# Newton rounds of the early RMS norms on GpSimd, halves of the squares added there, pairs 2 and 3 normalized singly, first exponents earlier

## The chip, the cores and the metric

The kernel runs on one core of a Trainium2 chip. The core has five engines with instruction queues of their own: TensorE (PE, with its weight loads PEld), VectorE (DVE), ScalarE (ACT), GpSimd (POOL) and SyncE (SP, which here only issues DMAs). Each runs its queue strictly in order and waits on semaphores of the others. The metric is device time in microseconds (us), the median of several executions. One execution with the hardware profiler gave the profile.

## The reference

Three stages in a row, all in float32; the MLP's weights arrive as 64-bit floats, and the kernel converts them itself.

```python
# q, k, v: (4 batches, 12 heads, 448 positions, 64)
rms = np.sqrt(np.mean(x * x, axis=-1, keepdims=True) + 1e-06)
q_n, k_n = q / rms_q * g_q, k / rms_k * g_k
scores = (1 / 8) * q_n @ k_n.T              # per head, 448 x 448
attn = np.exp(scores - max); attn = attn / (attn.sum() + 1e-09)
x = (attn @ v) -> (1792, 768)
h = x @ w_in                                # 768 -> 2048
x = (h * np.clip(h + 3, 0, 6) / 6) @ w_out  # 2048 -> 768
# capacity MoE: logits = x @ w_gate; greedy assignment, 224 tokens for each of 8 experts
out[expert e's tokens] = np.maximum(x @ w1[e], 0) @ w2[e]
```

## The kernel before

The 48 (batch, head) units are worked on as 24 pairs of heads, `i` = 0 to 23, six to a batch. Pairs 0 to 5 are the first batch. Nothing of the MLP can run beside them, since it needs all heads of a batch; from the second batch on, MLP matmuls of the batch before fill PE between the attention steps. Beside the first batch, DVE and ACT also convert `w_in` from 64 bits to 32 (`conv`, lines 140 to 143, tile `cv`, which has one buffer: the next conversion waits until the store of the last one has landed).

For each pair: squares of q and k on ACT (`sq`, two buffers), their sums over 64 columns on DVE (`sums`, L253: 16 sums per position-partition, 8 for q and 8 for k); the inverse root from a bit-trick guess (L257, L258) and three Newton rounds of three small dependent instructions (L260 to L262) on DVE (`invert`); the scaling of q and k on GpSimd (`norm`, L273, tile `xn`, one buffer each for q and k); transposes on PE (`transp`, L290), split into a rounded high part on ACT (`qh`, `kh`) and a low part on DVE (`ql`, `kl`, L302); rough scores on PE (`s1`, L313) for the row maxima on DVE (`mx`, L316, eight per pair); the maxima transposed (`mt`, L322) and spread by DVE (`mr`, L324); exact transposed scores (`sT`, L335) with that maximum subtracted, exponents on ACT (`ph`, L346), and attention times v on PE (`av`, L375). In the first batch the output's scaling is: row sums (`scol`, L390) and their reciprocal (L395) on DVE, the product on GpSimd (`num`, L396), then transposes on PE (L407).

All PSUM tiles come from one ring of eight banks, in program order.

The order on every engine is written out by hand. Each step of pair `i` has a due time in slots, counted from 16 x `i` (the `T_...` tables); events are sorted by due time, and at each slot the queued MLP matmuls are dealt out between them. So a pair takes 16 slots, and a step's due time alone sets where it stands in every engine's queue. In the table before, `sums` of a pair stand at -50, `invert` at -42, `norm` at -38, the q and k transposes at -30 and -28, `sT` at 0, 0.1, 8, 8.1, and `normalize` (which holds the L395 and L396 instructions) at 28. Pairs 0 and 1 have a Newton chain each; from pair 2 on, two neighbouring pairs share one (`GROUPS`), with 32 columns instead of 16.

Of the kernel before, what the change touches and what calls it, by code (L numbers as in the profile page):

```python
# [8 lines left out]
F32 = mybir.dt.float32  # L9
F32R = mybir.dt.float32r  # L10
BF16 = mybir.dt.bfloat16
I32 = mybir.dt.int32
AF = mybir.ActivationFunctionType
OP = mybir.AluOpType
# [7 lines left out]
def kernel(  # L22
# [14 lines left out]
    nc = tc.nc  # L37
    B, H, S, D = q.shape
# [5 lines left out]
    CP = 112  # L44
    NCH = S // CP
# [9 lines left out]
    SQ = 2  # L55
# [12 lines left out]
    CI, CI0, CI1, CI2, CO = 6, 1.75, 2.5, 0.5, 1.5  # L68

    T_LOAD, T_VLOAD, T_NORM, T_Q, T_K, T_V = -72, -12, -38, -30, -28, 6  # L70
    T_SUMS, T_INV = -50, -42
    T_S1, T_MT = (-24, -23.9, -16, -15.9), -9
    T_ST = (0, 0.1, 8, 8.1)
    T_AV = ((17, 18, 19.5, 20.5), (22, 23, 24.5, 25.5))
# [120 lines left out]
    apool = a_stack.enter_context(tc.tile_pool(name="apool", bufs=2, side="left"))  # L195
# [23 lines left out]
    QKV, OPER, XT, FIRST, TR = {}, {}, {}, {}, {}  # L219
    NH2 = B * H // 2  # L220
# [16 lines left out]

    NST = 2 * 2 * NCH

    GROUPS = [(0,), (1,)] + [(g, g + 1) for g in range(2, NH2, 2)]  # L240
    GROUP = {i: g for g in GROUPS for i in g}
    ST = {}

    def sums(i):

        g = GROUP[i]
        if g not in ST:
            ST[g] = [apool.tile([CP, len(g) * NST], F32, name=f"st{k}_{len(g)}", bufs=2) for k in range(3)]
        o = g.index(i) * NST
        for a in range(2):  # L250
            sq = apool.tile([CP, 2 * NCH, D], F32, name="sq", bufs=SQ)
            nc.scalar.activation(sq, QKV[i][a].rearrange("p h c d -> p (h c) d"), AF.Square)
            nc.vector.tensor_reduce(ST[g][0][:, o + a * 2 * NCH:o + (a + 1) * 2 * NCH], sq, axis=AX.X, op=OP.add)  # L253

    def invert(g):
        ms, y, t = ST[g]
        nc.vector.tensor_scalar(ms, ms, 1.0 / D, 1e-6, op0=OP.mult, op1=OP.add)  # L257
        nc.vector.tensor_scalar(y.bitcast(I32), ms.bitcast(I32), -0.5, 1597463007.0, op0=OP.mult, op1=OP.add)  # L258
        for _ in range(3):
            nc.vector.scalar_tensor_tensor(t, y, -0.5, y, op0=OP.mult, op1=OP.mult)  # L260
            nc.vector.tensor_tensor(t, t, ms, op=OP.mult)
            nc.vector.scalar_tensor_tensor(y, t, 1.5, y, op0=OP.add, op1=OP.mult)  # L262

    def norm(i):
        g = GROUP[i]
        y = ST[g][1][:, g.index(i) * NST:(g.index(i) + 1) * NST]
        n = 2 * NCH
# [438 lines left out]
    def at(t, fn, *args):  # L706
        events.append((t, len(events), fn, args))
# [7 lines left out]
    for i in range(NH // 2):  # L715
        t = 16 * i
        at(t + T_LOAD, load, i)
        at(t + T_VLOAD, vload, i)
        g = GROUP[i]
        first = 16 * g[0]  # L720
        at(first + T_SUMS + 4 * (i - g[0]), sums, i)
        if i == g[-1]:
            at(first + T_INV, invert, g)
        at(t + T_NORM, norm, i)
        at(t + T_Q, transp, i, 0)
        at(t + T_K, transp, i, 1)
        at(t + T_V, vsplit, i)
        for c in range(NCH):
            at(t + (T_S1[c] if i else -24 + 0.1 * c), s1, i, c)
            at(t + T_ST[c], sT, i, c)  # L730
            if i in QMAJOR:
                for s in range(2):
                    at(t + T_AV[s][c], av, i, s, c)
            else:
                at(t + T_PV[c], pv, i, c)
        at(t + (T_MT if i else -21), mt, i)
        if i in QMAJOR:
            at(t + T_NUM, normalize, i)
            at(t + T_XT, xt, i)
        else:  # L740
            for n in range(2):
                at(t + T_ADD[n], padd, i, n)
            for d, fn in ((T_SUM, psums), (T_RS, rs_out), (T_RL, rs_in), (T_REC, rec), (T_RO, r_out), (T_RB, r_in), (T_X, xmul)):
                at(t + d, fn, i)
            at(t + T_XH, xsplit, i, False)
            at(t + T_XL, xsplit, i, True)
        if (i + 1) % NP == 0:
            at(t + T_MLP[i // NP], mlp_next, i // NP)
# [315 lines left out]
    for t in range(NTC):  # L1064
        a, z = t * 128, t * 128 + 128
# [137 lines left out]
    for pi, (t, hfs) in enumerate(passes):  # L1203
# [10 lines left out]
        for f in range(NF):  # L1214
            i, k = divmod(f, QF)
# [139 lines left out]
```

## Time and profile before

| | us |
|---|---|
| runs of the kernel, median of 3 | 1167.9 (1166.67 to 1169.88) |
| the profiled execution's own time | 1170.09 |
| its span, first to last instruction | 1168.3 |
| busy in the span: PE | 1104.3 (95%) |
| DVE | 716.6 (61%) |
| ACT | 518.7 (44%) |
| POOL | 426.3 (36%) |

PE is busy nearly throughout, so what PE loses at any place tends to reach the end. In the page's 40 slices of 29 us PE's busy tenths begin 3, 8, 8, 8, 9 and DVE's 7, 8, 8, 7, 8: the first 115 us, the first batch, are where PE has gaps and DVE is fullest.

### The profile page before, as it was taken

To read this page: it belongs to the slowest core of one execution; us is meant where nothing else is said; L and a number is where in the kernel's file an instruction comes from. 1 tells how busy PE (TensorE), PEld (TensorE's weight loads), DVE (VectorE), ACT (ScalarE), POOL (GpSimd) and SP (SyncE) were. 2 spreads that over 40 slices of the span, in tenths; PEclk is the share of its full clock that TensorE was granted. 3 is DMA by queue.
4 is the path that set the end of the run, shared out by engine and by line. 5 is a ranking of instruction groups with operands and counts; after the bars stand their busy time and mean duration, and the time that the engine had idled before them with its cause. 6 is when DMAs were issued, how large, how long until landed. Compare 5 with 4: busy or idle time off the path is not lost.

```text
span 1168.3 us, 19514 instructions
## 1 busy us (share of the span) xinstructions
PE 1104.3 (95%) x7253; PEld 908.8 (78%) x7253; DVE 716.6 (61%) x1493; ACT 518.7 (44%) x941; POOL 426.3 (36%) x317
## 2 busy tenths in 40 slices
PE   3888989999999999999999999999998899999997
PEld 2777756756766666788777888888877899999997
DVE  7887887886667755213440666666665866666560
ACT  3655645644545546544452111111114765656551
POOL 2322455664444532213353000000004676865550
PEclk9998989999999999999999999999998899999999
DMA  4465898978677777759996323222237887877731
GB/s 122 119 190 137 251 293 262 311 236 313 219 240 237 251 263 260 231 195 305 312 350 188 80 61 83 69 82 69 72 91 198 232 259 227 253 228 220 227 127 41
DMA packets 212679, 230.96 MB, mean 198 GB/s; under 512 B 26276, under 2 KB 185704, under 8 KB 212584
## 3 DMA queue, kind: packets, MB, share of 16 engines
q1 hardware_dynamic: 209256, 218.71, 60.9%
q0 software_dynamic: 3328, 11.01, 3.1%
q8 instruction: 57, 0.93, 0.3%
q14 instruction: 38, 0.31, 0.1%
HBM read 178.63 MB, written 51.04 MB: 197 GB/s over the span
## 4 chain that ended last, share of the span: by engine, by line
PE 69%; DVE 10%; DMA 9%; issue 5%; ACT 4%; POOL 2%; SPq 1%; POOLq 0%; DVEq 0%; ACTq 0%
PE y L1155 19%; PE h L528 15%; PE y L1307 8%; PE h L1243 6%; PE st L335 4%; PE h L1245 3%; PE av L424 3%; PE av L375 2%; DMA w_hl<-w 2%; DMA sum_dr<-rb 2%; DVE cv L142 1%; PE rt L948 1%; PE lg L570 1%; DVE mx L316 1%; ACT ph L346 1%
## 5 line engine op out<-in xcount | busy, mean ns | idle before, releaser
L528 PE MATMUL h<-xh,w 128*128 128x448 f32 x768 | 242.3, 386 | 2.8 <-DVE mr L324 2.3
L528 PEld LDWEIGHTS h<-xh,w 128*128 128x128 f32 x768 | 144.5, 192 | 38.6 <-issue 22.2
L528 PE MATMUL h<-xl,w 128*128 128x448 f32 x384 | 146.7, 382 | 0.0
L316 DVE TENSOR_REDUCE mx<-s 112x1 f32<-112x448 f32 x192 | 105.8, 612 | 41.6 <-PE s L313 41.5
L1093 ACT ACTIVATE g2h<-gr 128x512 fp32r<-128x512 f32 x60 | 37.7, 631 | 205.9 <-PE y L1155 160.5
L1155 PE MATMUL y<-woh,g2l 128*128 128x512 f32 (+1 forms) x448 | 125.1, 345 | 1.2 <-POOL g2l L1058 1.2
L1155 PE MATMUL y<-woh,g2h 128*128 128x512 f32 (+1 forms) x448 | 125.4, 345 | 0.0
L1155 PE MATMUL y<-wol,g2h 128*128 128x512 f32 (+1 forms) x448 | 125.1, 344 | 0.0
L118 DVE TENSOR_TENSOR wel<-we_s,weh 128x768 fp32r<-128x768 f32 x59 | 89.3, 1520 | 55.6 <-ACT weh L117 43.7
L117 ACT ACTIVATE weh<-we_s 128x768 fp32r<-128x768 f32 x107 | 88.3, 841 | 63.1 <-DMA we_s<-in_moe_w_dram 45.5
L118 POOL TENSOR_TENSOR wel<-we_s,weh 128x768 fp32r<-128x768 f32 x48 | 97.3, 2031 | 49.8 <-ACT weh L117 36.4
L346 ACT ACTIVATE ph<-st 112x448 f32<-112x448 f32 x192 | 92.6, 543 | 41.6 <-PE st L335 40.7
L1243 PE MATMUL h<-xe,weh 128*128 128x448 f32 x318 | 102.2, 381 | 3.7 <-DVE xe L1194 3.7
L1058 POOL TENSOR_TENSOR g2l<-gr,g2h 128x512 fp32r<-128x512 f32 x14 | 18.2, 1304 | 232.3 <-ACT g2h L1093 232.2
L417 POOL TENSOR_TENSOR pa<-ph 112x448 f32<-112x448 f32 x68 | 84.7, 1267 | 47.4 <-ACT ph L346 47.4
L528 PEld LDWEIGHTS h<-xl,w 128*128 128x128 f32 x384 | 74.0, 193 | 12.3 <-issue 7.0
L1155 PEld LDWEIGHTS y<-woh,g2h 128*128 128x128 f32 x448 | 72.0, 189 | 10.8 <-issue 1.5
L1155 PEld LDWEIGHTS y<-woh,g2l 128*128 128x128 f32 x448 | 72.0, 189 | 10.7 <-POOL g2l L1058 1.4
L1155 PEld LDWEIGHTS y<-wol,g2h 128*128 128x128 f32 x448 | 71.9, 189 | 9.1 <-issue 0.7
L531 ACT ACTIVATE r<-h,half 128x448 f32<-128x448 f32 x64 | 40.6, 635 | 83.2 <-PE h L528 73.0
L1245 PE MATMUL h<-xe,wel 128*128 128x224 f32 x318 | 77.5, 271 | 0.0
L1307 PE MATMUL y<-weh,hl 128*112 128x384 f32 x216 | 72.9, 338 | 0.0
(245 smaller groups left out, 2346.7 us busy)
## 6 DMA issues: line engine op xcount, KB each, us to landing
we_s<-in_moe_w_dram SPq DMA_DIRECT2D x128, 384.0 KB
w<-w_hl SPq DMA_DIRECT2D x32, 768.0 KB
gr<-g_dr SPq DMA_DIRECT2D x52, 256.0 KB
wraw<-in_moe_w_in_dram SPq DMA_DIRECT2D x16, 768.0 KB
win_v<-w SPq DMA_DIRECT2D x32, 384.0 KB
w_hl<-w SPq DMA_DIRECT2D x16, 768.0 KB
wraw<-in_moe_w_out_dram SPq DMA_DIRECT2D x16, 768.0 KB
g_dr<-g SPq DMA_DIRECT2D x48, 224.0 KB
```

Of the source, the lines that this page charges most:

```text
L117: nc.scalar.activation(hi, raw, AF.Copy)
L118: eng.tensor_tensor(lo, raw, hi.bitcast(F32), op=OP.subtract)
L316: mx = nc.vector.tensor_reduce(MX[i][:, s, c:c + 1], pp[s][:CP, :S], axis=AX.X, op=OP.max)
L335: nc.tensor.matmul(pp[s][:CP, :S], a[r], b[r], start=(n == 0), stop=(n == len(todo) - 1))
L346: nc.scalar.activation(e, pp[s][:CP, :S], AF.Exp)
L417: nc.gpsimd.tensor_tensor(PA[i, s, n], PP[i, s, 2 * n][0], PP[i, s, 2 * n + 1][0], op=OP.add)
L528: nc.tensor.matmul(p[:, :S], lhs[:, c], x[:, c], start=(n == 0), stop=(n == 3 * NC - 1))
L531: nc.scalar.activation(r, p[:, :S], AF.Relu, bias=half, scale=1.0 / 6.0)
L1155: nc.tensor.matmul(pp[hf][:, :COLS[hf].stop - COLS[hf].start], a[:, f % QF], w[:, COLS[hf]], start=(f == 0 and n == 0), stop=(f == NF - 1 ...
L1243: mm = [lambda: nc.tensor.matmul(p[:, :4 * CP], wh[:, fo], x.rearrange("d k t -> d (k t)"), start=(c == 0), stop=(c == NC - 1), skip_group ...
L1245: lambda: nc.tensor.matmul(p[:, :2 * CP], wl[:, fo], x[:, 0], start=False, stop=False, skip_group_check=True)]
L1307: nc.tensor.matmul(p[:CP, :HW], a[:, f, tk], w[:, o], start=(f == 0 and n == 0), stop=(f == FB - 1 and n == 2))
```

## The change

For pair groups that begin at pairs 1 to 9, the three Newton rounds move from DVE to GpSimd, where a round takes four instructions (the fused DVE forms are written out). The guess stays on DVE. Pairs 2 and 3 now form groups of their own. For the groups (4,5), (6,7), (8,9) the rounds stand at -35.5, just behind `normalize` of the pair four before, and the scaling of the group's first pair right behind them at -35.4. For pairs 2 to 9 GpSimd first adds the two halves of each pair's squares (`fold`), so that DVE sums 32 columns instead of 64; squares, fold and sums now stand at three due times. The first pair's exact scores and exponents move from slots 0, 0.1, 8, 8.1 to -9, -8.9, 1, 1.1.

```diff
-    GROUPS = [(0,), (1,)] + [(g, g + 1) for g in range(2, NH2, 2)]
+    GROUPS = [(g,) for g in range(4)] + [(g, g + 1) for g in range(4, NH2, 2)]
+    def squares(i):
+        for a in range(2):
+            SQS[i, a] = apool.tile([CP, 2 * NCH, D], F32, name="sq", bufs=SQ)
+            nc.scalar.activation(SQS[i, a], QKV[i][a].rearrange("p h c d -> p (h c) d"), AF.Square)
+
+    def fold(i):
+        for a in range(2):
+            sq = SQS[i, a]
+            nc.gpsimd.tensor_tensor(sq[:, :, :D // 2], sq[:, :, :D // 2], sq[:, :, D // 2:], op=OP.add)
+            SQS[i, a] = sq[:, :, :D // 2]
+    def guess(g):                       # the two instructions that invert() began with, on DVE
+    def invert(g):
+        ms, y, t = ST[g]
+        if 0 < g[0] < NG0:              # NG0 = 10
+            p = nc.gpsimd
+            for _ in range(3):
+                p.tensor_tensor(t, y, y, op=OP.mult)
+                p.tensor_tensor(t, t, ms, op=OP.mult)
+                p.tensor_scalar(t, t, -0.5, 1.5, op0=OP.mult, op1=OP.add)
+                p.tensor_tensor(y, y, t, op=OP.mult)
+            return
-        at(first + T_SUMS + 4 * (i - g[0]), sums, i)
+        t_sq = first + T_SUMS + 4 * (i - g[0])
+        at(t_sq, squares, i)
+        if 2 <= i < NG0:
+            at(t_sq + 2, fold, i)
+            t_sq += 3
+        at(t_sq, sums, i)
+        late_g = 4 <= g[0] < NG0
         if i == g[-1]:
-            at(first + T_INV, invert, g)
-        at(t + T_NORM, norm, i)
+            at(t_sq if 2 <= i < NG0 else first + T_INV, guess, g)
+            at(first + (T_INV0 if late_g else T_INV), invert, g)     # T_INV0 = -35.5
+        at(t + (T_INV0 + 0.1 if late_g and i == g[0] else T_NORM), norm, i)
-            at(t + T_ST[c], sT, i, c)
+            at(t + (T_ST[c] if i else (-9, -8.9, 1, 1.1)[c]), sT, i, c)
```

On GpSimd before, around the output scaling of pair 0 (`num`): the scalings of pair 4 (`xn_615`, `xn_617`) stand ahead of it.

```order
L273 TENSOR_TENSOR xn_428<-ld_q,st_2_252 112x2x4x64
L273 TENSOR_TENSOR xn_430<-ld_k,st_2_252 112x2x4x64
L273 TENSOR_TENSOR xn_615<-ld_q,st_2_433 112x2x4x64
L273 TENSOR_TENSOR xn_617<-ld_k,st_2_433 112x2x4x64
L396 TENSOR_TENSOR num<-num,scol 112x512
L273 TENSOR_TENSOR xn_792<-ld_q,st_2_433 112x2x4x64
```

On GpSimd now, the same place: the folds of pairs 4 and 5, `num` of pair 0, and behind it the first of three Newton rounds of pairs 4 and 5.

```order
L254 TENSOR_TENSOR sq<-sq 112x8x32 x4
L419 TENSOR_TENSOR num<-num,scol 112x512
L277 TENSOR_TENSOR st_2_514<-st_2_513 112x32
L278 TENSOR_TENSOR st_2_514<-st_2_514,st_2_512 112x32
L279 TENSOR_SCALAR st_2_514<-st_2_514 112x32
L280 TENSOR_TENSOR st_2_513<-st_2_513,st_2_514 112x32
```

On GpSimd now, eight rows on, the end of the third round and what stands behind it: the scalings of pair 4 (`xn_653`, `xn_655`) and 5.

```order
L278 TENSOR_TENSOR st_2_514<-st_2_514,st_2_512 112x32
L279 TENSOR_SCALAR st_2_514<-st_2_514 112x32
L280 TENSOR_TENSOR st_2_513<-st_2_513,st_2_514 112x32
L296 TENSOR_TENSOR xn_653<-ld_q,st_2_513 112x2x4x64
L296 TENSOR_TENSOR xn_655<-ld_k,st_2_513 112x2x4x64
L296 TENSOR_TENSOR xn_826<-ld_q,st_2_513 112x2x4x64
L296 TENSOR_TENSOR xn_828<-ld_k,st_2_513 112x2x4x64
```

So pair 4's scaling moved from ahead of `num` to behind it and behind twelve dependent instructions; pairs 6 and 8 stand the same way behind `num` of pairs 2 and 4.

On DVE before, ahead of pair 2's `mr`: two of the conversion's instructions with the guess and, in between, the Newton rounds of pairs 4 and 5 (the first is shown).

```order
L390 TENSOR_SCALAR scol<-av,eps 112x4
L141 TENSOR_SCALAR cv<-cv 128x768
L257 TENSOR_SCALAR st_2_432<-st_2_432 112x32
L258 TENSOR_SCALAR st_2_433<-st_2_432 112x32
L260 SCALAR_TENSOR_TENSOR st_2_434<-st_2_433 112x32
L261 TENSOR_TENSOR st_2_434<-st_2_434,st_2_432 112x32
L262 SCALAR_TENSOR_TENSOR st_2_433<-st_2_434,st_2_433 112x32
```

On DVE now, the same place: the sums of pair 5's folded squares, the guess, and then `mr` without the nine Newton instructions.

```order
L413 TENSOR_SCALAR scol<-av,eps 112x4
L265 TENSOR_REDUCE st_2_512<-sq 112x8 x2
L269 TENSOR_SCALAR st_2_512<-st_2_512 112x32
L270 TENSOR_SCALAR st_2_513<-st_2_512 112x32
L141 TENSOR_SCALAR cv<-cv 128x768
L142 SCALAR_TENSOR_TENSOR cv<-wraw,cv 128x768
L347 TENSOR_TENSOR mr<-t,place 128x448
```

The nine rows between the guess and `mr` are gone from DVE's queue, here and at the other four groups.

## Rows read from the trace of the kernel before

**Rows 1.** Busy time by stretch: us, then each engine's busy time (instructions), granted clock, DMA

```profile
40.00:50.00 10.00, 8.00 (x64) 6.71 (x65) 8.98 (x25) 4.43 (x9) 3.65 (x3) 0.86 0.20 51
```

**Rows 2.** PE's waits, 0 to 115 us: us in total, times, longest

```profile
PE s L313 <- DVE mr L324: 5.2, 3, 2.3
```

**Rows 3.** DVE in time: start, us, instruction, count, idle before it and what ended it

```profile
13.67 0.18 DVE L260 SCALAR_TENSOR_TENSOR st<-st 112x16 f32<-112x16 f32 x1
...
15.44 4.33 DVE L316 TENSOR_REDUCE mx<-s 112x1 f32<-112x448 f32 x8
...
39.48 1.27 DVE L253 TENSOR_REDUCE st<-sq 112x8 f32<-112x512 f32 x2
...
42.27 0.19 DVE L260 SCALAR_TENSOR_TENSOR st<-st 112x32 f32<-112x32 f32 x1
...
44.19 0.95 DVE L142 SCALAR_TENSOR_TENSOR cv<-wraw,cv 128x768 int32<-128x768 int32 x1
...
49.15 0.20 DVE L395 RECIPROCAL scol<-scol 112x8 f32<-112x8 f32 x1
51.05 0.56 DVE L141 TENSOR_SCALAR cv<-cv 128x768 int32<-128x768 int32 x1 [1.70 <-ACT cv L140]
```

**Rows 4.** DVE in time, the same columns, later in the first batch

```profile
78.91 0.20 DVE L395 RECIPROCAL scol<-scol 112x8 f32<-112x8 f32 x1
...
111.31 0.22 DVE L390 TENSOR_SCALAR scol<-av,eps 112x4 f32<-112x4 f32 x1 [1.87 <-PE av L375]
...
113.25 0.20 DVE L395 RECIPROCAL scol<-scol 112x8 f32<-112x8 f32 x1
```

**Rows 5.** GpSimd in time, the output scalings of pairs 0, 2 and 4

```profile
49.61 1.06 POOL L396 TENSOR_TENSOR num<-num,scol 112x512 f32<-112x512 f32 x1 [1.85 <-ACT num L391]
...
79.42 1.06 POOL L396 TENSOR_TENSOR num<-num,scol 112x512 f32<-112x512 f32 x1 [1.53 <-ACT num L391]
...
113.61 1.63 POOL L396 TENSOR_TENSOR num<-num,scol 112x512 f32<-112x512 f32 x1 [4.55 <-ACT ph L346]
```

**Rows 6.** PE in time: three stalls, and the q transposes of pairs 4, 6, 8

```profile
45.73 0.46 PE L313 MATMUL s<-kh,qh 64*112 64x448 f32 x2 [2.00 <-DVE mr L324]
...
53.58 0.55 PE L290 MATMUL t<-ident,xn 112*128 112x112 f32 x4
...
65.14 0.60 PE L407 MATMUL t<-ident,num 112*128 112x112 f32 x4 [1.29 <-POOL num L396]
...
76.21 0.45 PE L313 MATMUL s<-kh,qh 64*112 64x448 f32 x2 [2.26 <-DVE mr L324]
...
84.03 0.55 PE L290 MATMUL t<-ident,xn 112*128 112x112 f32 x4
...
117.37 0.55 PE L290 MATMUL t<-ident,xn 112*128 112x112 f32 x4
```

**Rows 7.** Granted clock behind two stalls: us, PE's busy time, clock, DMA

```profile
49.00:50.00 1.00, 1.00 (x10) 0.50 0.81 187
66.00:67.00 1.00, 1.00 (x13) 1.00 0.82 192
```

**Rows 8.** GpSimd and DVE lines: count, durations in ns (least, median, most)

```profile
L474 POOL TENSOR_TENSOR xl<-xn_t,xh x17: 1137/1158/2194, 158.3 to 509.7; 128x448 fp32r<-128x448 f32 x17
...
L118 DVE TENSOR_TENSOR w<-win_v,w x16: 946/959/3446, 128.8 to 591.5; 128x768 fp32r<-128x768 f32 x16
...
L118 POOL TENSOR_TENSOR w<-win_v,w x16: 1824/1842/1860, 129.7 to 587.0; 128x768 fp32r<-128x768 f32 x16
```

**Rows 9.** A small GpSimd instruction: busy us, mean ns, idle before

```profile
L845 POOL IOTA ei<- 128x8 int32 x1 | 0.2, 154 | 0.0
```

**Rows 10.** GpSimd in time, one weight split

```profile
138.48 1.83 POOL L118 TENSOR_TENSOR w<-win_v,w 128x768 fp32r<-128x768 f32 x1 [7.01 <-ACT w L117]
```

**Rows 11.** DVE in time beside it, a guess of 32 columns

```profile
139.74 0.61 DVE L257 TENSOR_SCALAR st<-st 112x32 f32<-112x32 f32 x1
140.39 1.08 DVE L258 TENSOR_SCALAR st<-st 112x32 int32<-112x32 int32 x1
```

**Rows 12.** ACT in time, pair 2's output copied out

```profile
78.91 0.38 ACT L391 ACTIVATE num<-av 112x256 f32<-112x256 f32 x1 [3.83 <-DVE scol L390]
```

**Rows 13.** The chain that ended last: start, us, what

```profile
154.00 9.09 DMA w_hl<-w
```

More of the change, by code (lines that the diff above doesn't have):

```diff
@@ L70 @@
     T_LOAD, T_VLOAD, T_NORM, T_Q, T_K, T_V = -72, -12, -38, -30, -28, 6
-    T_SUMS, T_INV = -50, -42
+    T_SUMS, T_INV, T_INV0, NG0 = -50, -42, -35.5, 10
     T_S1, T_MT = (-24, -23.9, -16, -15.9), -9
@@ L238 @@
     NST = 2 * 2 * NCH
-    GROUPS = [(0,), (1,)] + [(g, g + 1) for g in range(2, NH2, 2)]
+    GROUPS = [(g,) for g in range(4)] + [(g, g + 1) for g in range(4, NH2, 2)]
     GROUP = {i: g for g in GROUPS for i in g}
     ST = {}
+    SQS = {}
+    def squares(i):
[7 more added lines that the diff above has]
+            SQS[i, a] = sq[:, :, :D // 2]
     def sums(i):
@@ L250, in sums @@
         for a in range(2):
-            sq = apool.tile([CP, 2 * NCH, D], F32, name="sq", bufs=SQ)
-            nc.scalar.activation(sq, QKV[i][a].rearrange("p h c d -> p (h c) d"), AF.Square)
+            sq = SQS.pop((i, a))
             nc.vector.tensor_reduce(ST[g][0][:, o + a * 2 * NCH:o + (a + 1) * 2 * NCH], sq, axis=AX.X, op=OP.add)
-    def invert(g):
+    def guess(g):
         ms, y, t = ST[g]
```

## The prediction

> **What bounds the kernel now.** I read the page's busy slices first, then the table of stretches, PE's waits, the timelines of DVE, PE and GpSimd, and last the chain of waits. PE is busy for 95% of the span, and from the second batch on MLP matmuls fill its gaps, so only the first batch is in question. There DVE is the fullest engine: from 40 to 50 us it works 8.98 of 10 us, GpSimd 3.65, and PE 8.00 at a granted clock of 0.86 [rows 1]. The sharpest place is pair 2's `mr`: PE waited for such a spread of maxima three times, 5.2 us in all [rows 2]. The timeline says why. At 42.27 DVE begins the Newton rounds of pairs 4 and 5 and is through at 44.19; `mr` stands behind them, and PE's next rough scores start at 45.73 after 2.00 us idle [rows 3, 6]. The same happens at 76.21, with 2.26 us [rows 6]. After the first of these stalls PE has a clock of 0.50 for a while; after a stall of 1.29 us at 65.14 it keeps 1.00 [rows 6, 7]. So a Newton chain on DVE costs its own length and some clock behind it.
>
> **What the change takes off DVE.** A chain of nine is 15.44 - 13.67 = 1.77 us for 16 columns and 44.19 - 42.27 = 1.92 us for 32 [rows 3]; four chains have 32 columns. Two reductions of 512 columns take 1.27 us; a column costs 4.33 / 8 / 448, a little over 1 ns, so halving saves about 0.27 us each, 0.54 per pair [rows 3]. I cut the path at the reciprocals of pairs 0, 2 and 4 (49.15, 78.91, 113.25) [rows 3, 4].
>
> Up to 49.15: Newton 1.77 + 1.92 + 1.92, halves for four pairs 2.2, less one guess more (two instructions of 1.92 / 9) 0.4: 7.4 us off DVE. Not all of it reaches the path, since pairs 1 to 3 now hang on a serial GpSimd queue: Newton, two scalings, two folds. Pair 1's Newton, now begun where DVE's began (13.67), ends at about 16.5, its scalings at 18.6, pair 2's folds at 20.1 (prices below), while DVE is ready for pair 2's sums at about 19.2: it has mx done at 13.67 + 4.33 and `mr` a microsecond later [rows 3]. That wait, with the sum's own place, costs 0.7; PE then runs pair 0's two early exponent sets before pair 1's scores, for which I put 1.0; and 0.3 for each fold of pairs 3 to 5. So 7.4 - 2.6 = 4.8, and I take **4.7 us gained** (between 3.2, if each GpSimd instruction costs what the second rival says, and 7.4). The early exponents themselves cost nothing: ACT has worked 4.43 us of ten even later [rows 1]; what they gain, an earlier release of PSUM banks, I put at nothing, because DVE's eight maxima per pair, 4.33 us, come behind it anyway.
>
> From 49.15 to 78.91: 1.92 and one pair's halves 0.54 (the other pair's stand beside a wait for ACT): **2.5**. From 78.91 to 113.25: 1.92 + 0.54, and the 1.87 us that DVE waited for `av` at 111.31, which ran at half clock behind the Newton stall [rows 4]: **4.3**. In all 11.5 us.
>
> **What it puts behind `num`.** In the order of GpSimd, pair 4's scaling has moved from ahead of pair 0's `num` to behind it and behind twelve instructions, each of which waits for the one before. Behind these wait pair 4's and 5's scalings and the next `num`; PE's q transposes of pair 4 wait for the first of them, and PE is in order, so all of PE waits, and with it DVE's `ql`. No DMA is passed. No row shows GpSimd on 16 or 32 columns. From 448 columns in 1158 ns and 768 in 1842 [rows 8], a column costs 2.14 ns and an instruction 0.20 us: 0.27 us for 32 columns, 0.235 for 16, 0.75 for a fold of 256. The one-input instruction I put at the 0.154 us of the small iota [rows 9]. A chain of twelve is then 9 x 0.27 + 3 x 0.154 = 2.9 us (2.6 for 16 columns). Bounds: all at 0.154, 1.85 us; or with 0.13 us more for each wake, which is what GpSimd took from the end of ACT's copy (79.29) to `num` (79.42) [rows 5, 12], 4.45 us. I take 2.9, the value nearest the rows that compute.
>
> GpSimd and DVE also exclude each other: an instruction of the guess on DVE, of a size that otherwise takes 0.19 us [rows 3], lasted from 139.74 to 140.35, just until GpSimd's split of 138.48 to 140.31 ended, and the next one 1.08 us [rows 10, 11]. So the conversion on DVE, 0.56 + 0.95 us for two instructions [rows 3] and 2.46 for three, holds up the chain where it falls into it: two beside pair 4's chain, all three beside pair 6's, one beside pair 8's.
>
> From a reciprocal's start to the q transposes, now: wait for `num` 0.46, 0.51, 0.36; `num` 1.06, 1.06, 1.63 [rows 5]; chain 2.9; exclusion 1.5, 2.5, 0.95; one scaling 1.1 (it has `num`'s size). Sums 7.0, 8.1, 6.9. Before: 53.58 - 49.15 = 4.4, 84.03 - 78.91 = 5.1, 117.37 - 113.25 = 4.1 [rows 3, 4, 6]. **8.4 us lost.** It doesn't hide: in between PE has only `xt` and one `av` block to do.
>
> **Clock.** PE's new stalls are of over 3 us, longer than the 2.00 that lost the clock. In 40 to 50 us the clock of 0.86 cost 1.4 us [rows 1]; three times that, **4.2 us lost** (nothing, if the stalls stay near 1.29).
>
> Sum: -11.5 + 8.4 + 4.2 = +1.1. On the profiled execution's own 1170.1 us that is 1171.2; its own time stands 2.2 above the median of the runs, so **1169.0**. What a measurement of this kernel can tell from no change is about 0.3%, 3.5 us: the forecast is no change that can be told, 1165.5 to 1172.5.
>
> **Rivals.**
> *The chain is short and the clock stays* (faster). For it: the small iota's 0.154 us, and DVE's fullness [rows 1, 9]. Against it: two-input instructions have an offset of 0.20 by the line through rows 8. With 1.85 us a chain, three tails are 3.2 shorter (5.2), the first leg gains 0.7 more, stalls come near 2 us and the clock holds: -12.2 + 5.2 = -7.0, so 1160.9.
>
> *The Newton chain behind `num` becomes the wait that sets the pair's pace* (slower). At 4.45 us a chain the tails lose 13.0, the first leg gains 3.2 in place of 4.7, so -10.0 + 13.0 + 4.2 = +7.2: 1175.1. It decides from about 0.29 us an instruction on, where the sum passes +3.5. For it: twelve waits in series, and the wake of 0.13. Against it: DVE's own chain loses only 0.02 us between instructions (1.92 / 9 against 0.19) [rows 3]. The Trainium skill's GPSIMD Engine Reference (Elementwise, side-by-side cycle accounting) measures GpSimd at 1.96 times DVE's time for an add and keeps to DVE for elementwise work. At 768 columns this trace has 1842 ns against 959, 1.92 times, as the page says [rows 8]; for 32 columns no run here shows it. By that ratio on DVE's 0.19 us an instruction would be 0.37 us, and the sum that of this rival, as an estimate.
>
> *The difference is swallowed downstream* (no change, 1167.9). The chain of waits goes through a 9.09 us transfer at 154.00 [rows 13]: if weight traffic sets the pace there, up to 9 us of either sign could vanish. Against it: those transfers are issued by the same slots and would move with them.
>
> **How the numbers follow.** Forecast 0.36, short chain 0.30, long chain 0.25, swallowed 0.09. Of the forecast a little lies beyond 3.5 us on either side, and of the short chain some lies within: faster 0.33, same 0.40, slower 0.27. The range reaches to both outer rivals, 1160 to 1176; the forecast's own is given above.
>
> **What would show it.** Right: GpSimd's twelve in 2.6 to 3.5 us behind `num`; PE's longest waits in the first batch at the q transposes of pairs 4, 6, 8, ended by GpSimd, 2.5 us or more each; no wait for `mr`; pair 0's reciprocal near 44.5; a clock of 0.5 behind the transposes. Wrong: a chain under 2 us or PE waits under 1.5 us there (then the first rival), or a chain over 4 us, and DVE waiting for folds in pairs 2 and 3 for more than 2 us (the second).

## The result and the profile after

| | before | after |
|---|---|---|
| median (lowest to highest) of 4 runs each | 1168.89 (1166.67 to 1171.38) | 1184.01 (1179.16 to 1185.31) |
| profiled execution's own time | 1170.09 | 1182.85 |
| span | 1168.3 | 1181.1 |
| mean granted clock over the span | 0.977 | 0.969 |

The ratio is 1.014 (95% interval 1.0101 to 1.0178): 15 us slower, where 1169.0 with a range of 1160 to 1176 was forecast. Measured once more later, the kernel gave 1184.57 and 1.0147 (1.0107 to 1.0187).

I read the same stations as in the prediction: the reciprocals of pairs 0, 2 and 4, the q transposes of pairs 4, 6 and 8 behind them, and one more that closes each tail, the next transposed maxima (of pairs 3, 5, 7). First GpSimd in time in after, from pair 0's `num` to pair 4's first scaling (start, us, instruction, idle before it).

```profile
45.62 1.06 POOL L419 TENSOR_TENSOR num<-num,scol 112x512 f32<-112x512 f32 x1 [7.11 <-ACT num L414]
46.64 0.24 POOL L277 TENSOR_TENSOR st<-st 112x32 f32<-112x32 f32 x1
46.95 0.25 POOL L278 TENSOR_TENSOR st<-st,st 112x32 f32<-112x32 f32 x1
...
48.10 0.24 POOL L277 TENSOR_TENSOR st<-st 112x32 f32<-112x32 f32 x1
48.42 1.53 POOL L278 TENSOR_TENSOR st<-st,st 112x32 f32<-112x32 f32 x1
...
51.33 1.06 POOL L279 TENSOR_SCALAR st<-st 112x32 f32<-112x32 f32 x1
52.47 0.25 POOL L280 TENSOR_TENSOR st<-st,st 112x32 f32<-112x32 f32 x1
52.80 1.04 POOL L296 TENSOR_TENSOR xn<-ld_q,st 112x512 f32<-112x512 f32 x1
```

DVE in time in after, the reciprocals, and beside the chain the conversion's instructions:

```profile
45.16 0.20 DVE L418 RECIPROCAL scol<-scol 112x8 f32<-112x8 f32 x1
...
48.90 0.94 DVE L142 SCALAR_TENSOR_TENSOR cv<-wraw,cv 128x768 int32<-128x768 int32 x1
...
51.37 0.94 DVE L143 SCALAR_TENSOR_TENSOR cv<-wraw,cv 128x768 int32<-128x768 int32 x1
55.60 0.68 DVE L325 SCALAR_TENSOR_TENSOR ql<-t,gq,qh 128x448 fp32r<-128x448 f32 x1 [3.30 <-ACT qh L322]
...
83.32 0.20 DVE L418 RECIPROCAL scol<-scol 112x8 f32<-112x8 f32 x1
...
123.42 0.20 DVE L418 RECIPROCAL scol<-scol 112x8 f32<-112x8 f32 x1
```

The chain lasts from 46.64 to the scaling's start at 52.80, 6.2 us. An undisturbed instruction is busy for 0.22 to 0.25 us, and the next starts 0.30 to 0.34 us after its start. The two long ones, 1.53 and 1.06 us, end within 0.12 us of the end of the two 0.94 us conversion instructions on DVE (49.84 and 52.31).

PE in time in after: the q transposes of pairs 4, 6 and 8, each with the transposed maxima that come next.

```profile
53.89 1.01 PE L313 MATMUL t<-ident,xn 112*128 112x112 f32 x4 [3.88 <-POOL xn L296]
...
56.85 4.61 PE L398 MATMUL av<-vv,ph 112*112 112x66 f32 x24
61.26 0.39 PE L345 MATMUL t<-ident,mx 112*128 112x112 f32 x1
...
91.40 1.01 PE L313 MATMUL t<-ident,xn 112*128 112x112 f32 x4 [1.91 <-POOL xn L296]
...
98.77 0.39 PE L345 MATMUL t<-ident,mx 112*128 112x112 f32 x1
...
131.04 1.00 PE L313 MATMUL t<-ident,xn 112*128 112x112 f32 x4 [3.43 <-POOL xn L296]
...
138.41 0.39 PE L345 MATMUL t<-ident,mx 112*128 112x112 f32 x1
```

In before, PE in time had these two rows in the same place behind the first of these transposes:

```profile
55.10 2.48 PE L375 MATMUL av<-vv,ph 112*112 112x66 f32 x24
57.42 0.26 PE L322 MATMUL t<-ident,mx 112*128 112x112 f32 x1
```

The transposes took 0.55 us [rows 6] and take 1.01, and 24 blocks of `av` took 2.48 us and take 4.61. That is the clock, as PE's stretches of 2 us in after say (us, PE busy, clock, DMA share, GB/s):

```profile
48.00:50.00 2.00, 2.00 (x20) 1.00 0.10 30
50.00:52.00 2.00, 0.01 (x1) 0.57 0.00 0
52.00:54.00 2.00, 0.11 (x1) 0.50 0.40 105
54.00:56.00 2.00, 2.00 (x12) 0.50 1.04 251
...
62.00:64.00 2.00, 2.00 (x14) 0.52 0.00 0
64.00:66.00 2.00, 2.00 (x22) 1.00 0.00 0
```

PE has nothing to do from 50 to 53.9, the clock falls to 1.2 GHz (0.50) within that time and stays there for ten more microseconds in which PE is busy throughout. The stretches of 10 us in after show this three times, once behind each tail (columns as in [rows 1], which has 40 to 50 us of before):

```profile
40.00:50.00 10.00, 7.91 (x72) 6.42 (x68) 7.96 (x16) 5.40 (x11) 3.93 (x7) 1.00 0.41 120
50.00:60.00 10.00, 6.12 (x35) 6.11 (x34) 3.90 (x7) 2.17 (x4) 6.39 (x10) 0.51 0.68 183
...
90.00:100.00 10.00, 8.60 (x47) 8.26 (x49) 2.38 (x5) 2.95 (x5) 4.35 (x5) 0.56 0.56 143
...
130.00:140.00 10.00, 8.96 (x49) 8.56 (x51) 4.33 (x7) 2.97 (x5) 6.16 (x6) 0.50 0.93 242
```

Two more half-clock stretches of after, from about 81 to 88 us and from 118.5 to 125, stand behind other waits:

```profile
79.94 0.46 PE L336 MATMUL s<-kh,qh 64*112 64x448 f32 x2 [1.01 <-DVE mr L347]
...
116.21 1.00 PE L358 MATMUL st<-qh,kh 64*112 64x448 f32 x2 [1.50 <-DVE kl L325]
```

With the stations the whole difference up to pair 7's maxima is laid out (us; tails are from a reciprocal to the q transposes, spans from the transposes to the maxima, legs from the maxima to the next reciprocal):

| | before | after | change | forecast |
|---|---|---|---|---|
| start to pair 0's reciprocal | 49.15 | 45.16 | -4.0 | -4.7 |
| three tails | 4.4, 5.1, 4.1 | 8.7, 8.1, 7.6 | +10.8 | +8.4 |
| three spans | 3.84, 3.85, 3.84 | 7.37, 7.37, 7.37 | +10.6 | +4.2 (clock) |
| leg of pair 2 | 21.49 | 22.06 | +0.6 | -2.5 |
| leg of pair 4 | 25.37 | 24.65 | -0.7 | -4.3 |
| pair 7's maxima at | 121.2 | 138.4 | +17.2 | +1.1 |

At the end of the span 12.8 us of the 17.2 are left in these two executions.

A second reading needs only what every run has, its span and its mean clock. Span x (1 - clock) is the time that the clock was short of: about 22 us in before (median of 31 runs), 37.8 in after. It also counts stretches in which PE had nothing to do, so it is an upper bound; it is given as "deficit" below.

### The profile page after: what moved, and what is told of

The parts are those of the page before. It is cut to its first block, busy times and chain, and to the rows that moved or that the text cites. A ratio compares the mean times of both kernels' runs of the same rounds, so it can differ in the third digit from the quotient of the medians.

```text
span 1181.1 us, 19559 instructions
## 1 busy us (share of the span) xinstructions
PE 1114.9 (94%) x7253; PEld 916.6 (78%) x7253; DVE 698.4 (59%) x1450; ACT 518.8 (44%) x941; POOL 456.0 (39%) x405
## 4 chain that ended last, share of the span: by engine, by line
PE 69%; DVE 8%; DMA 7%; issue 5%; POOL 5%; ACT 4%; SPq 1%; POOLq 0%; DVEq 0%; ACTq 0%
PE y L1185 19%; PE h L551 16%; PE y L1337 8%; PE h L1273 5%; PE st L358 4%; PE av L447 3%; PE av L398 3%; PE h L1275 3%; DMA w_hl<-w 2%; PE rt L978 1%; PE lg L593 1%; DMA we_s<-in_moe_w_dram 1%; PE t L313 1%; PE sm L457 1%; DVE cv L142 1%
## 5 line engine op out<-in xcount | busy, mean ns | idle before, releaser
L118 DVE TENSOR_TENSOR wel<-we_s,weh 128x768 fp32r<-128x768 f32 x59 | 86.2, 1469 | 54.8 <-ACT weh L117 42.5
L1185 PEld LDWEIGHTS y<-woh,g2l 128*128 128x128 f32 x448 | 72.0, 189 | 10.6 <-POOL g2l L1088 1.3
```

Of the source, the lines that this page charges most:

```text
L118: eng.tensor_tensor(lo, raw, hi.bitcast(F32), op=OP.subtract)
L1185: nc.tensor.matmul(pp[hf][:, :COLS[hf].stop - COLS[hf].start], a[:, f % QF], w[:, COLS[hf]], start=(f == 0 and n == 0), stop=(f == NF - 1 ...
```

## Experiments

Two theories went in. One: the stalls cost mainly the clock that they lose, and holding the clock gives the time back with the chain left where it is. The other: the chain is in PE's way by its own length, and only moving or shortening it helps. A third said that the first batch matters little for the end.

**late_dve**: the late groups' rounds back on DVE, at their old place.

```diff
-        if 0 < g[0] < NG0:
+        if 0 < g[0] < 4:
...
-        late_g = 4 <= g[0] < NG0
+        late_g = False
```

> The changed kernel, but the Newton rounds of the groups (4,5), (6,7), (8,9) are back on DVE at -42, and their scalings back at -38; folds, single groups 2 and 3 and the early exponents stay. Theory A (the chain behind num and the half clock after it cost the time): the q transposes of pairs 4, 6, 8 wait for nothing, their tails from the reciprocal are 4 to 5 us again, and the kernel comes out 3 to 6 us faster than the one before, near 1164. Rival B (folds, single groups or early exponents cost it too): it stays above 1172. Rival C (all gains of the start are lost further on): within 2 us of the one before.

1168.3 us, ratio 1.0003 (0.9985 to 1.0021), deficit 26.8. 16 us of the loss are gone, and the old wait is back. One row of PE's waits in late_dve from 0 to 140 us (total, times, longest):

```profile
PE s L336 <- DVE mr L347: 6.9, 3, 2.9
```

So the loss lies in the late groups' chains and where they stand, not in the folds, the single groups or the early exponents, which this kernel keeps. The 3 to 6 us ahead of before that theory A forecast did not come. That it only equals before, though its reciprocals come at 47.27, 77.87 and 112.75 (before 49.15, 78.91, 113.25), is what the third theory would also say.

**late_front**: the rounds stay on GpSimd, but stand ahead of `num`.

```diff
-        late_g = 4 <= g[0] < NG0
+        late_g = False
```

> The changed kernel, but the late groups' GpSimd rounds stand at -42 and their scalings at -38, so ahead of num and not behind it. Theory A (it is the place behind num): pair 4's scaling is ready when PE comes, num is late by 1 to 2 us instead, no half clock of 10 us; 1163 to 1169. Rival B (GpSimd as such: twelve small instructions at 0.33 us and the exclusion by the conversion, wherever they stand): num is late by 4 us or more, PE waits there, and the time stays above 1177.

1170.57 us, ratio 1.002 (0.9992 to 1.0049), deficit 31.6. The tails are 6.2, 4.5 and 4.2 us. But now `num` comes late, and PE waits for that; PE in time in late_front, pair 0's output transposes:

```profile
48.97 0.60 PE L430 MATMUL t<-ident,num 112*128 112x112 f32 x4 [2.60 <-POOL num L419]
```

Behind them PE's stretch of 10 us in late_front, busy throughout at half clock:

```profile
50.00:60.00 10.00, 10.00 (x59) 0.53 0.67 184
```

Position matters (13 to 14 us against after), and the stall that is left still took the clock in the profiled execution, whose time was the longest of its ten (1176.83).

**warm**: after, unchanged but for 16 added matmuls ahead of each of the three q transposes, into the bank that the transposes then overwrite.

```diff
         t = ps.tile([128, 512], F32, name="t", tag="b", bufs=8)
+        if which == 0 and i in (4, 6, 8):
+            qh, _, kh, _ = OPER[i - 1]
+            for _ in range(16):
+                nc.tensor.matmul(t[:CP, :S], qh[:, :CP], kh, start=True, stop=True)
```

> The changed kernel with 16 matmuls of 448 columns more in each of the three stalls, ahead of the q transposes of pairs 4, 6 and 8, into the bank that the transposes then overwrite; the chain on GpSimd is as long as before. Theory A1 (two thirds of the loss at these places is PE's half clock after the stall, 10.6 us over the three): the granted clock stays at 1.00 behind the transposes, from the q transposes to the next transposed maxima it is again 3.9 us instead of 7.4, and the kernel is 8 to 14 us faster than the changed one, 1170 to 1175. Rival A2 (the stalls themselves are the loss): the time stays within 4 us of the changed one, 1180 to 1187.

1165.28 us, ratio 0.9992 (0.9966 to 1.0017), deficit 15.7: 17 to 19 us less than after (by the ratios to before, and by the medians), with more work on PE. PE in time in warm:

```profile
49.68 3.45 PE L315 MATMUL t<-kh,qh 128*112 128x448 f32 x16
54.07 0.60 PE L317 MATMUL t<-ident,xn 112*128 112x112 f32 x4 [0.95 <-POOL xn L296]
...
57.97 0.26 PE L349 MATMUL t<-ident,mx 112*128 112x112 f32 x1
```

PE's stretches of 2 us in warm, where after had 0.50:

```profile
52.00:54.00 2.00, 1.12 (x6) 1.00 0.47 130
54.00:56.00 2.00, 1.93 (x20) 1.00 0.96 259
56.00:58.00 2.00, 2.00 (x23) 1.00 1.06 354
```

The tails are as long as in after (8.8, 8.1, 7.6 us), the q transposes at 54.07 even stand 0.2 later. With the chain as it was, the clock is what differs, and the maxima come 3.9 us behind the transposes, as before. This is the run that decides: more than the 8 to 14 us came back that I had expected. By pair 7's maxima 9.9 us are back in these executions (128.53 in warm, 138.41 in after), near the 10.6 of the three spans. The rest came later in the run, where warm's clock was also less short (a deficit of 8.0 us from there on, 12.7 in after, 17.7 in before); nothing here ties that part to the added matmuls. Half-clock stretches that the added matmuls don't cover stay (0.60 from 70 to 80 us, 0.55 from 110 to 120).

**one_round**: one Newton round instead of three in the late groups.

```diff
-            for _ in range(3):
+            for _ in range(3 if g[0] < 4 else 1):
```

> The changed kernel with one Newton round instead of three in the groups (4,5), (6,7), (8,9), so two rounds of each are left out. Theory A: the chain is 1.3 us instead of 4.0 to 5.8, PE's waits at the q transposes fall to 1 us or less, the clock holds, and the time is 1160 to 1167. Rival A2 (the stalls alone, without the clock): three times 3 us off, 1173 to 1177. Rival B: above 1178.

1165.52 us, ratio 0.9999 (0.9973 to 1.0025), deficit 24.4. The wait at pair 4's q transposes shrinks, and the clock is lost even so in the profiled execution, whose time was the longest of its ten (1174.44); PE in time in one_round:

```profile
50.51 0.76 PE L313 MATMUL t<-ident,xn 112*128 112x112 f32 x4 [0.78 <-POOL xn L296]
```

PE's stretch of 10 us around it:

```profile
50.00:60.00 10.00, 9.49 (x53) 0.54 0.66 186
```

In time, a chain of a third is about as good as late_dve's. It doesn't tell the theories apart by itself, since a shorter chain is a shorter stall too.

**few**: as warm, with 6 matmuls for 16.

```diff
+            for _ in range(6):
```

> The changed kernel with 6 added matmuls (about 1.3 us) instead of 16 ahead of the q transposes of pairs 4, 6 and 8, so that over 2 us of idle time stay in each stall. Theory A (an idle stretch of 2 us or more loses the clock, as it did at 45.73 and 76.21 before the change): the clock still falls in most of them, 1174 to 1184. Rival (any work in the stall holds the clock): 1164 to 1169 as with 16.

1173.98 us, ratio 1.0061 (1.0037 to 1.0084), deficit 26.4: between after and warm, at the edge of theory A's range. The profiled execution took 1191.28 us, 17 above the median, so only the total is used here.

**after_again** is the kernel after without an edit, measured beside few.

> The changed kernel itself, so that it stands on the same chip as the two above: 1179 to 1186 by every theory.

1184.57 us, deficit 38.4, waits of 4.28, 4.10 and 3.45 us at the three transposes: the loss repeats.

**no_conv**: what the conversion on DVE adds to the chain.

```diff
-            for part in (0, 1, 2, 3, C_ST):
+            for part in (0, 1, 2, 3, C_ST) if out_ else (0, C_ST):
```

> The changed kernel without the three DVE instructions of each conversion of w_in, which are left out. Exclusion theory: the chain of twelve behind num takes 12 x 0.33 = 4.0 us at all three places, in place of 6.1, 5.5 and 4.6, and no instruction of it is over 0.3 us. Rival (the long ones among the twelve are GpSimd's own): single instructions of 0.9 to 1.5 us stay.

A single execution, 1156.74 us, to be read for the chain alone. GpSimd in time in no_conv, behind pair 0's `num`:

```profile
44.93 0.24 POOL L277 TENSOR_TENSOR st<-st 112x32 f32<-112x32 f32 x1
...
48.16 0.22 POOL L279 TENSOR_SCALAR st<-st 112x32 f32<-112x32 f32 x1
48.46 0.25 POOL L280 TENSOR_TENSOR st<-st,st 112x32 f32<-112x32 f32 x1
48.78 1.04 POOL L296 TENSOR_TENSOR xn<-ld_q,st 112x512 f32<-112x512 f32 x1
```

Twelve take 48.78 - 44.93 = 3.85 us, 0.32 each, and none is longer than 0.25. So beside the conversion the three chains lose 2.3, 1.7 and 0.7 us (6.2, 5.5 and 4.6 in after). PE's three waits are 2.44, 2.45 and 2.45 us, and behind the first the clock is 0.50 from 50 to 60 us.

**front_warm**: late_front with added matmuls ahead of the output's transposes, where its stalls are.

```diff
+        qh, _, kh, _ = OPER[min(i + 2, NH2 - 1)]
+        for _ in range((5, 10)[i % 2 == 0] if i < NP else 0):
+            nc.tensor.matmul(t[:CP, :S], qh[:, :CP], kh, start=True, stop=True)
```

> The kernel with the late rounds ahead of num (late_front), and in the first batch 448-column matmuls ahead of the output transposes of each pair (10 for even pairs, 5 for odd ones), in the bank that the transposes then overwrite, where late_front's PE waited 1.3 to 2.6 us for num. Theory (what is left of the loss is half clock after these waits): the clock holds from 45 to 130 us but for single microseconds, and the time is 1157 to 1163, below both kernels. Rival (the added matmuls displace work, 2 us a pair where PE does not wait): 1166 to 1173.

1158.12 us, ratio 0.9931 (0.9907 to 0.9956), deficit 13.3: faster than both kernels. PE's stretches of 10 us in front_warm:

```profile
40.00:50.00 10.00, 8.34 (x68) 1.00 0.41 120
50.00:60.00 10.00, 10.00 (x100) 1.00 0.65 186
...
100.00:110.00 10.00, 8.29 (x48) 0.74 0.62 165
```

From 50 to 60 us PE ran 100 matmuls where late_front ran 59. The reciprocals come at 45.13, 75.06 and 109.90: 4.0, 3.9 and 3.4 us ahead of before.

**front_warm2** is the same kernel once more, measured beside **dve_warm**, which has the same added matmuls with the late rounds on DVE:

```diff
-        if 0 < g[0] < NG0:
+        if 0 < g[0] < 4:
```

> front_warm once more, beside the two above on one chip: 1156 to 1160, 0.993 of the kernel before.

> front_warm with the rounds of the groups (4,5), (6,7), (8,9) on DVE at -42; folds, GpSimd rounds of pairs 1 to 3, early exponents and the matmuls ahead of the output transposes stay. Theory (with the clock held, DVE's 1.9 us per group count): 4 to 7 us slower than front_warm, 1162 to 1166. Rival (with the clock held, it does not matter which engine has the late rounds): within 2 us of front_warm.

1159.89 (0.9926, 0.9902 to 0.9951; deficit 16.2) and 1161.38 (0.9958, 0.9936 to 0.998; deficit 16.3). The intervals overlap; with the clock held, no engine for the late rounds is shown to be the better one.

**before_warm**: before, with 9 added matmuls in the last exact-score block of pairs 1, 3 and 5.

```diff
+        for _ in range(9 if c == 3 and i in (1, 3, 5) else 0):
+            nc.tensor.matmul(pp[0][:CP, :S], qh[:, :CP], kh, start=True, stop=True)
```

> The kernel before, with 9 matmuls of 448 columns more in pairs 1, 3 and 5 ahead of the last chunk of exact scores (in its bank, which the scores then overwrite), just ahead of PE's waits for mr at 45.73, 76.21 and 107.38; nothing of the change. Theory (half clock after these waits cost the kernel before as well, about 1.4 us in two places and up to 5 in the third): the clock holds there, 2 to 7 us faster than before, 1159 to 1164. Rival (the kernel before is bound by DVE there, so PE's clock does not matter): within 2 us of before.

1162.11 us, ratio 0.9962 (0.9933 to 0.999), deficit 13.3. The kernel before paid for the clock too: part of what front_warm gains is there without any move of the rounds. The profiled execution was the longest of its twelve (1174.3), so that the clock held is read from the deficit alone. The intervals of before_warm, dve_warm, front_warm and front_warm2 overlap: with added matmuls on both sides, no gain of the moved rounds, the folds and the early exponents over before is shown.

**early_only**: before, with the first pair's scores and exponents early.

```diff
-            at(t + T_ST[c], sT, i, c)
+            at(t + (T_ST[c] if i else (-9, -8.9, 1, 1.1)[c]), sT, i, c)
```

> The kernel before with the first pair's exact scores and exponents early (-9, -8.9, 1, 1.1) and nothing else. As I put it, they gain and cost nothing: pair 0's reciprocal within 0.5 us of 49.15. Rival (PE's two early sets, at half pace, hold up pair 1's scores): 1 to 2 us later.

A single execution, 1169.5 us; pair 0's reciprocal at 48.96 instead of 49.15. On this leg the part costs and gains nothing that shows, as forecast.

## Why the prediction was wrong

The step that failed is the clock: "three times that, **4.2 us lost**". I had priced a stall at what the half clock cost inside one stretch of before, 1.4 us. It is 3.5 us per stall up to the next maxima alone (7.37 - 3.84), 10.6 for three, and it doesn't end there. An estimate for the whole way to pair 7's maxima is PE's busy time x (1 - clock), summed over stretches of 1 us: 8.1 us in before, 20.5 in after. So about 12.4 of the 17.2 us are the clock's, where 4.2 were forecast; PE's idle time grew by 2.6 (29.6 to 32.1), and some 2 us are not assigned. The deficits of all runs differ by 37.8 - 22.1 = 15.7 us (an upper bound), the medians by 15 to 18, and warm, with the chain in place and its waits filled, gives 17 to 19 back.

Each of the three waits, of 1.9 to 3.9 us, lost PE half its speed for some ten busy microseconds. What I took as the price was a short stretch, about 3.4 us at half clock from 47.3 on [rows 1, 7]. The same trace has a long one, from about 105.3 to 115.5 us, and I passed it over; stretches of 10 us in before:

```profile
100.00:110.00 10.00, 7.47 (x48) 5.48 (x47) 9.06 (x24) 3.68 (x9) 2.04 (x2) 0.77 0.53 140
110.00:120.00 10.00, 9.98 (x75) 8.68 (x75) 6.97 (x12) 5.21 (x10) 5.67 (x5) 0.72 0.39 94
```

These two lost 2.3 + 2.8 = 5.1 us, not 1.4. A second term failed as well: the legs of pairs 2 and 4 were to gain 6.8 us and gained 0.1.

Step by step:

- *Leg to pair 0's reciprocal*: right (-4.0 for -4.7). The chain for 16 columns had 0.297 us an instruction, where I had put 0.235 for a two-input one; 4.0 lies between the term's 4.7 and its lower end of 3.2. Halving saved 0.27 us a reduction, as put, though 4.33 / 8 / 448 us a column would have given 0.31. DVE waited for folds for 2.2 us in all, but for 1.5 in pairs 2 and 3, under the 2 us that I had named as a sign of the second rival.
- *Legs of pairs 2 and 4*: -2.5 and -4.3 forecast, +0.6 and -0.7 measured. The Newton chains did leave DVE, but nearly all of the gain was gone, and DVE's time turned into waits: 11.1 us for `qh` from 45 to 140. By the same estimate in stretches of 0.5 us, half clock took 2.5 us of pair 2's leg (0.5 in before), while PE's idle time in it fell from 3.8 to 2.5. In front_warm, where the clock holds there, this leg takes 19.76 us (55.30 to 75.06), 1.7 less than in before: most of the 2.5. In pair 4's leg 1.87 us were to come back because the half clock "behind the Newton stall" would go. But in before it began at about 105.3, ahead of that stall (0.91 us, ended at 107.38) and behind another wait, and after has the same kind of wait at 116.21; PE in time in before:

```profile
104.38 1.00 PE L335 MATMUL st<-qh,kh 64*112 64x448 f32 x2 [1.53 <-DVE kl L302]
```

  Half clock took 3.5 us of this leg in before and 3.8 in after, so that part of the gain did not come.
- *Tails*: 7.0, 8.1, 6.9 forecast, 8.7, 8.1, 7.6 measured; the mechanism and the place were right, the size 2.4 us short. The chain alone is 3.85 us, not 2.9. The busy times of the twelve do add up to 2.9, by luck: a two-input instruction took 0.24 or 0.25 us where the line through two large sizes gave 0.27, a one-input one 0.22 where I put 0.154. The sum lacked the 0.08 us from the end of one to the start of the next, 1.0 us in twelve. The second rival's condition (from 0.29 us an instruction on) was met; with its 4.45 and my clock it gave 1175.1, so the clock was too small there too. The Trainium skill's ratio of 1.96 (GPSIMD Engine Reference, Elementwise) had given 0.37 by estimate; measured 0.32 it is an overestimate, on the right side of the line.
- *Exclusion by the conversion*: 4.95 us forecast in all, 4.7 measured; no_conv shows that it is the conversion. By place 1.5, 2.5 and 0.95 were forecast and 2.3, 1.7 and 0.7 measured, so that the sum fits is partly luck. The Trainium skill (SBUF — State Buffer, Who interferes with whom) has a DVE instruction with two SBUF inputs contend with a GpSimd instruction that reads SBUF, over a shared port pair whose use it calls an exclusive lock; the 0.25 us instruction that took 1.53 beside a 0.94 us one agrees.
- *Waits*: "no wait for `mr`" was nearly right (1.7 us from 0 to 140 where there were 5.2 [rows 2]), but 1.0 of it stands ahead of the half clock from 81 us on. The waits at the transposes of pairs 4 and 8 were over 2.5 us as said, and 1.91 at pair 6's.
- *Swallowed downstream*: 17.2 us at pair 7 became 12.8 at the end of one pair of executions, about a quarter less, and the medians differ by 15 to 18: most is not swallowed. But warm, 7.3 us behind before at pair 7's maxima (128.53 against 121.21), ends 2.6 ahead of it; how much of a delay in the first batch reaches the end depends on the clock further on and isn't settled here.

The Trainium skill (TensorE: Matmul & The Clock Gate, HAM oscillation) tells of a loop that loses the clock anew at every wait and pays for it at each step. The trace agrees at the three chains, with 0.51, 0.56 and 0.50 behind them; not every wait did this (1.25 us ahead of 70.14 in after, and 1.00 from 70 to 80).

What stays open: which wait loses the clock. The length of a single wait doesn't tell. In before 1.29 us kept it [rows 6, 7] and 2.00 lost it; in after_again a wait of 1.27 us that ended at 71.58 was followed by 0.50 from 74 us on; one of no_conv's three waits of 2.45 us kept it for 2 us more. The same kernel's executions also differ by up to 16 us (late_front 1160.96 to 1176.83, with deficits of 19.7 and 42.3), so some of these losses come or stay away by chance. The folds and the single groups were not run alone.

## What to carry to other kernels

Price a new TensorE wait by what follows it, not by its length: here 1.9 to 3.9 us of waiting cost 3.5 us more in the next stretch, and three groups of otherwise useless matmuls in the gaps gave back 17 to 19 of 1184 us. Compare runs by span x (1 - mean clock) before looking for a cause elsewhere. And before moving a dependent chain to a slower engine, look at who stands behind it in that queue, and measure the pitch from one start to the next, not the busy time.

## What the hardware showed that I had not expected

- With PE idle for 3.9 us, the clock was at 0.50 before PE's next matmul, and stayed for some ten microseconds in which PE was busy for all of the time.
- Added matmuls made kernels faster: three groups of 16 took 3.45 us each and saved 17 to 19 us; in before three groups of 9 saved 4 to 6 (ratio 0.9962; 1167.86 to 1162.11).
- Twelve small dependent GpSimd instructions take 3.85 us for 32 columns and 3.57 for 16 (13.59 to 17.16 us): at this size the columns hardly count.
- A GpSimd instruction of 0.25 us was recorded as starting at 48.42, 0.48 us ahead of the conversion's at 48.90, and still ended behind it; the earlier recorded start did not decide which of the two went first.
